# A tuned Fourier-mixing and gated-MLP kernel: one weight third loaded and folded inside stage 1, small pieces of work in other steps, the next batch's stage 2 earlier

## The chip, the cores and the metric

One core of a Trainium2 chip. The metric is the device time of one execution in microseconds (us). A profiled execution gives a trace of every engine; its time axis starts at the first instruction.

## The reference, cut to what matters

```python
# x: (8, 3008, 256); w_gate, w_val: (256, 1536); w_out: (1536, 256)
X = np.fft.fft(np.fft.fft(x, axis=1), axis=2).real.reshape(24064, 256)
out = (np.maximum(X @ w_gate, 0) * (X @ w_val)) @ w_out
```

## The kernel before

The sequence transform is done in two stages of matmuls (3008 = 94 x 32). The feature transform is folded into the weights: `wc` and `ws` are the cosine and sine transforms of W_gate and W_val, made on the chip in three thirds of 512 columns, four folds to each third (gate and value, cosine and sine). A fold is two small f32 matmuls into one PSUM buffer (PSUM is the memory that TensorE writes) and a cast of the result by ScalarE. In the start, the eight pieces of batch 0's stage 1 are done in groups, the lower half of the sequence first and the upper half when that part of x has come; the first evacuation of a piece copies its result out of PSUM. After the start, 288 steps run: 8 batches, 3 blocks, 12 slices of the hidden width. Each does the gate and value products (G and V in the traces), direct and mirrored; the output products follow 12 steps later. Steps 0 to 11 also do the remaining eight folds and the rest of batch 0's stage 2, in small pieces of matmul and copy: `upright` turns a block by a permutation (pst), `rotate` mends one column of it (psr), `stage2` makes a cosine or a sine half of a block's result (ps, copied to pq). The Nyquist row of each block is written to DRAM and read back, broadcast over 128 partitions (`nb`). The parts concerned:

```python
# start: x pieces of batch 0, then the first third of both weights (POOL's queue)
load_first(0, 8); ...; load_first(24, 8); ...; load_first(8, 4); load_first(20, 4)
...; load_first(12, 4); load_first(16, 4); ...
load_w(0, pl)
...
group((1, 2, 3), False); warm(9)      # lower half of stage 1; fillers: matmuls whose result nobody reads
...                                   # tables on ScalarE, copies of x on VectorE and ScalarE
group((1, 2, 3), True)                # upper half, then first_evac(1), (2), (3)
...
group((4, 5), False); warm(4); ...; group((4, 5), True)
...
group((6, 7, 0), False); first_evac(4, "act")
nc.sync.dma_start(out=seen[:], in_=t1t[0][0:1, 0, 8:10])   # waits for first_evac(4)
load_w(1, nc.sync); load_w(2, nc.sync)                     # second and third thirds
... pair_w(0, 0, dve)                 # sum and difference of the halves of W_gate's third
group((6, 7, 0), True)
...
fold_w(0, 0, 0, g_tile()); upright(0, 0, "act"); upright(0, 1, "dve"); fold_w(0, 0, 1, psw)
...                                   # rotation, two stage-2 halves, two more folds

def fold_w(n, i, cs, ps=None):
    ps = ps or spare("psw")           # spare: the two "o" buffers in turn
    ...                               # two f32 matmuls of 64 columns by 512
    nc.scalar.copy((wc, ws)[cs][i][:, sl_], ps[:])
    if cs and (n or i): scale_w(n, i, ps)     # VectorE reads the same buffer

# batch b+1: stage 1, shuffle through DRAM, rotation, stage 2, at these steps of batch b
sh, tr, t2 = (22, 28, (29, 30, 32, 34, 35, 37)) if b else (25, 30, (31, 32, 33, 34, 35, 37))
for i, k in enumerate(t2):
    at(t0 + k, stage2, b + 1, i // 2, i % 2, "act")   # cosine half, then sine half
```

## Time and profile before

| | before |
|---|---|
| time, median of 3 runs | 625.5 us (625.27 to 626.45) |
| span of the profiled run | 623.2 us |
| last stage-1 matmul of batch 0 starts | 15.10 us |
| first gate matmul starts | 21.18 us |
| first output matmul (step 12) starts | 50.36 us |
| from there to the end of the span | 572.8 us |

The last four rows cut the run into three stretches: start, steps 0 to 11, rest.

### The profile page before, as it was taken

To read this page: it belongs to the slowest core of one execution; us is meant where nothing else is said; L and a number is where in the kernel's file an instruction comes from. 1 tells how busy PE (TensorE), PEld (TensorE's weight loads), DVE (VectorE), ACT (ScalarE), POOL (GpSimd) and SP (SyncE) were. 2 spreads that over 40 slices of the span, in tenths; PEclk is the share of its full clock that TensorE was granted. 3 is DMA by queue.
4 is the path that set the end of the run, shared out by engine and by line. 5 is a ranking of instruction groups with operands and counts; after the bars stand their busy time and mean duration, and the time that the engine had idled before them with its cause. 6 is when DMAs were issued, how large, how long until landed. Compare 5 with 4: busy or idle time off the path is not lost.

```text
span 623.2 us, 11964 instructions
## 1 busy us (share of the span) xinstructions
PE 614.0 (99%) x4284; PEld 409.6 (66%) x4284; DVE 538.2 (86%) x654; ACT 444.6 (71%) x855; POOL 519.9 (83%) x447
## 2 busy tenths in 40 slices
PE   8999999999999999999999999999999999999996
PEld 5336666766666666666667666666666666666665
DVE  8677997899889898888988998898988889899991
ACT  8667777777777767767677767767677776766661
POOL 8987998998989898998989989898988865565665
PEclk9999999999999999999999999999999999999998
DMA  7885274525553183613825255531832134212114
GB/s 169 240 161 118 61 191 113 137 66 160 118 139 84 34 235 83 151 36 89 212 75 126 64 158 123 135 90 34 226 89 49 34 85 117 60 34 67 34 35 100
DMA packets 42038, 67.44 MB, mean 108 GB/s; under 512 B 5877, under 2 KB 31774, under 8 KB 39962
## 3 DMA queue, kind: packets, MB, share of 16 engines
q1 hardware_dynamic: 37162, 50.61, 32.3%
q0 software_dynamic: 4656, 15.88, 10.7%
q8 instruction: 33, 0.54, 0.4%
q14 instruction: 27, 0.22, 0.1%
q10 hardware_dynamic: 160, 0.20, 0.1%
HBM read 38.85 MB, written 30.17 MB: 111 GB/s over the span
## 4 chain that ended last, share of the span: by engine, by line
PE 96%; DVE 2%; ACT 1%; issue 0%; POOL 0%; POOLq 0%; DVEq 0%
PE po L683 40%; PE V L634 20%; PE G L619 10%; PE G L620 10%; PE G L626 10%; PE psw L333 2%; PE ps L162 2%; PE ps L271 2%; DVE h L647 0%; PE pst L240 0%; PE ps L216 0%; ACT t L230 0%; ACT back L197 0%; PE ps L166 0%; DVE wm L327 0%
## 5 line engine op out<-in xcount | busy, mean ns | idle before, releaser
L654 POOL TENSOR_TENSOR h<-gm,E 128x992 bf16<-128x992 f32 (+1 forms) x138 | 320.1, 2319 | 81.8 <-DVE E L661 50.4
L683 PE MATMUL po<-wo,h 128*128 128x256 bf16 (+2 forms) x2304 | 328.5, 272 | 0.0
L683 PEld LDWEIGHTS <-h 128*128 128x128 bf16 (+2 forms) x2304 | 231.4, 103 | 105.9
L628 ACT ACTIVATE gm<-G 128x496 f32<-128x496 f32 (+1 forms) x288 | 170.6, 592 | 94.6 <-PE G L626 87.8
L647 DVE TENSOR_TENSOR h<-gs,V 128x1024 bf16<-128x1024 f32 (+3 forms) x150 | 173.8, 1159 | 58.7 <-PE V L634 39.7
L641 DVE SCALAR_TENSOR_TENSOR E<-nb,af,V 128x496 f32<-128x496 bf16 (+1 forms) x276 | 190.2, 731 | 2.2 <-PE G L620 2.2
L621 ACT ACTIVATE gs<-G 128x497 f32<-128x497 f32 (+2 forms) x288 | 169.6, 589 | 24.7 <-PE G L620 24.7
L661 DVE SCALAR_TENSOR_TENSOR E<-E,V 128x992 f32<-128x992 f32 (+1 forms) x138 | 164.5, 1192 | 0.0
L619 PE MATMUL G<-pq,wc 128*128 128x497 bf16 (+2 forms) x288 | 107.9, 375 | 0.0
L620 PE MATMUL G<-pq,ws 128*128 128x497 bf16 (+2 forms) x288 | 107.9, 375 | 0.0
L626 PE MATMUL G<-pq,wm 128*128 128x496 bf16 (+1 forms) x288 | 107.9, 375 | 0.0
L634 PE MATMUL V<-pq,ws 128*128 128x497 bf16 (+2 forms) x288 | 85.4, 375 | 0.9 <-DVE E L641 0.9
L634 PE MATMUL V<-pq,wc 128*128 128x497 bf16 (+2 forms) x288 | 85.4, 375 | 0.0
L620 PEld LDWEIGHTS <-ws 128*128 128x128 bf16 x288 | 28.2, 98 | 32.7
L696 ACT COPY os<-po 128x512 f32<-128x512 f32 x63 | 37.0, 587 | 14.6 <-PE po L683 12.6
L634 PEld LDWEIGHTS <-wc 128*128 128x128 bf16 x288 | 28.2, 98 | 20.0 <-issue 1.6
L114 POOL TENSOR_TENSOR eo<-xla 94x256 bf16<-94x256 f32 x56 | 40.4, 733 | 0.7
L619 PEld LDWEIGHTS <-wc 128*128 128x128 bf16 x288 | 28.2, 98 | 18.1 <-DVE pq L278 0.8
L114 POOL TENSOR_TENSOR eo<-xlb 94x256 bf16<-94x256 f32 (+1 forms) x42 | 34.5, 822 | 0.9
L111 POOL TENSOR_TENSOR xla<-xla,xha 94x510 f32<-94x510 f32 x28 | 32.9, 1175 | 2.2
L177 ACT CAST t<-ps 96x512 bf16<-96x512 f32 x56 | 32.7, 584 | 2.4 <-PE ps L162 0.2
L626 PEld LDWEIGHTS <-wm 128*128 128x128 bf16 x288 | 28.1, 98 | 4.1 <-issue 1.6
(142 smaller groups left out, 370.8 us busy)
## 6 DMA issues: line engine op xcount, KB each, us to landing
out_dram<-os SPq DMA_DIRECT2D x124, 128.0 KB
Td<-t SPq DMA_DIRECT2D x7, 768.0 KB
t<-Td SPq DMA_DIRECT2D x7, 768.0 KB
out_dram<-os SPq DMA_DIRECT2D x82, 64.0 KB
xla<-in_x_dram SPq DMA_DIRECT2D x7, 720.0 KB
xlb<-in_x_dram SPq DMA_DIRECT2D x6, 640.0 KB
nb<-Nd SPq DMA_DIRECT2D x23, 128.0 KB
out_dram<-os SPq DMA_DIRECT2D x40, 48.0 KB
```

The source lines that it names most:

```text
L114: yield eng.tensor_tensor(e1[:, :, k:k + H], x1[:, :, 0:H], free(x1, D, [DX, n], [-1, H]), op=op)
L619: nc.tensor.matmul(G[:, ds], lhsT=wc[0][:, fs], rhs=pq[:, 0, ds], start=True, stop=False)
L620: nc.tensor.matmul(G[:, ds], lhsT=ws[0][:, fs], rhs=pq[:, 1, ds], start=False, stop=True)
L621: nc.scalar.activation(pair(t, "gs")[:, t % 2, ds], G[:, ds], ACTF.Relu)
L626: nc.tensor.matmul(G[:, cols], lhsT=wm[0][:, f * 128:(f + 1) * 128], rhs=pqt[b, blk][:, 1, cols], start=False, stop=True, skip_group_check ...
L628: nc.scalar.activation(pair(t, "gm")[:, t % 2, cols], G[:, cols], ACTF.Relu)
L634: nc.tensor.matmul(pair(t, "V")[:, t % 2, cs], lhsT=w[:, f * 128:(f + 1) * 128], rhs=pqt[b, blk][:, min(k, 1), cs], start=(k == 0), stop=( ...
L641: nc.vector.scalar_tensor_tensor(pair(t, "E")[:, t % 2, cols], nbt[b, blk][:, cols], af[:, f:f + 1], pair(t, "V")[:, t % 2, cols], op0=ALU ...
L647: nc.vector.tensor_tensor(pair(t, "h")[:, k, 0, 0:ds.stop - ds.start], pair(t, "gs")[:, k, ds], pair(t, "V")[:, k, ds], op=ALU.mult)
L654: eng.tensor_tensor(free(pair(t, "h")[:], 1024 * (t % 2) + 512 + w - 1, [1024, n], [-1, w]), pair(t, "gm")[:, k, cols], val[:, k, cols], o ...
L661: nc.vector.scalar_tensor_tensor(E[:, :, cols], E[:, :, cols], 2.0, V[:, :, cols], op0=ALU.mult, op1=ALU.subtract)
L683: nc.tensor.matmul(po[0:m, i, :], lhsT=pair(t - f + ff, "h")[:, ff % 2, sg, g * 128:g * 128 + m], rhs=wo[:, ff, :], start=(ff == 0), stop= ...
```

## The change

The intent: fold one quarter of the first weight third in a stretch where TensorE runs fillers anyway; arrange small pieces so that two folds do not wait for one buffer; and get the next batch's stage 2 ready sooner. Cut to its core:

```diff
         load_first(0, 8)
+        load_w(0, pl, (0,))
 ...
-        load_w(0, pl)
+        load_w(0, pl, (1,))
 ...
-        warm(9)
+        warm(11)
 ...
+        absolute(dq[:], da[:]); cosines(cd...); sines(cd...)   # moved up
         nc.scalar.copy(w1[:, 1:10, :], wn[:, 1, 1:10, :])
+        pair_w(0, 0, dve)
+        fold_w(0, 0, 0, g_tile())                              # both moved up
 ...
-    for n in (1, 2):
-        for k, t in enumerate(((0, 1, 2, 3), (4, 5, 6, 7))[n - 1]):
-            at(t, fold_w, n, k // 2, k % 2)
-    ... upright at 2, 4, 6, 8; rotate at 3, 7; stage2 at 5, 9, 10, 11
+    for n in (1, 2):   # folds at the same steps 0 to 7
+        ... upright at 1, 2, 4, 6; rotate at 2, 6 (ahead of the fold); stage2 at 3, 5, 7, 8
-    plan = {0: (12, 13, 14, 16, 19, 22, 23, 24), ...
+    plan = {0: (12, 13, 14, 15, 17, 20, 21, 22), ...
-        sh, tr, t2 = ... (25, 30, (31, 32, 33, 34, 35, 37))
+        sh, tr, t2 = ... (23, 29, (30, 31, 32, 34, 35, 37))
-            at(t0 + k, stage2, b + 1, i // 2, i % 2, "act")
+            at(t0 + k, stage2, b + 1, i // 2, 1 - i % 2, "act")
-            for half, k in enumerate((5, 24) if b else (14, 31)):
+            for half, k in enumerate((5, 24) if b else (14, 26)):
```

Further: 17 instead of 15 fold pieces of batch 1's x before the steps, a slower pace after, and POOL's second x load ahead of the first fold piece.

More of the change, by code (lines that the diff above doesn't have):

```diff
@@ L20 @@
 WARM = 12
-FIRST = 15
+FIRST = 17
 def view(ap, offset, dims):
@@ L409 @@
         pl.iota(pi[:], pattern=[[0, 1]], base=0, channel_multiplier=1)
+        iota(pl, mi[:], [[0, 1]], 0, 1)
+        iota(pl, free(dd[:], 0, [64, 2], [1, 64]), [[1, 2], [2, 64]], 0, 0)
         load_first(8, 4)
         load_first(20, 4)
-        iota(pl, mi[:], [[0, 1]], 0, 1)
-        iota(pl, free(dd[:], 0, [64, 2], [1, 64]), [[1, 2], [2, 64]], 0, 0)
         load_first(12, 4)
@@ L450, in group, with g_tile @@
                     first_products(c, upper, k)
+        def g_tile():
+            return psg.tile([128, 512], F32, tag="g", name="psw")
         angles(0, 9)
@@ L466 @@
         nc.scalar.mul(wn[:, 0, 9:16, :], wn[:, 1, 9:16, :], -1.0)
-        nc.scalar.copy(w1[:, 1:10, :], wn[:, 1, 1:10, :])
         back(0, 2, "dve")
@@ L470 @@
         residue(da[:], dq[:], D, dve)
-        jj, sl, up, odd = bits(0, 15), bits(4, 1), bits(5, 3), bits(0, 1)
+        absolute(dq[:], da[:])
+        cosines(cd[:, 0, 1:H], dq[:, 1:H], D)
+        sines(cd[:, 1, 1:H], da[:, 1:H], D, 1.0)
+        nc.scalar.copy(w1[:, 1:10, :], wn[:, 1, 1:10, :])
+        odd = bits(0, 1)
+        dve.tensor_copy(cd[:, 1, 0:1], odd[:])
+        dve.tensor_scalar(cd[:, 0, 0:1], odd[:], scalar1=-1.0, scalar2=1.0, op0=ALU.mult, op1=ALU.add)
+        pair_w(0, 0, dve)
+        fold_w(0, 0, 0, g_tile())
+        jj, sl, up = bits(0, 15), bits(4, 1), bits(5, 3)
         ends(24, 8)
@@ L496 @@
         dve.tensor_scalar(tabs["wzn"][:], wz[:, 0], scalar1=-1.0, scalar2=None, op0=ALU.mult)
-        dve.tensor_copy(cd[:, 1, 0:1], odd[:])
-        dve.tensor_scalar(cd[:, 0, 0:1], odd[:], scalar1=-1.0, scalar2=1.0, op0=ALU.mult, op1=ALU.add)
         dve.tensor_scalar(ui[:], ui[:], scalar1=up[:], scalar2=-1.0, op0=ALU.is_equal, op1=ALU.mult)
@@ L510 @@
         dve.tensor_scalar(tis[:], tis[:], scalar1=NB - 1, scalar2=None, op0=ALU.bitwise_and)
-        absolute(dq[:], da[:])
-        cosines(cd[:, 0, 1:H], dq[:, 1:H], D)
-        sines(cd[:, 1, 1:H], da[:, 1:H], D, 1.0)
         group((6, 7, 0), False)
@@ L520 @@
         first_evac(5, "act")
-        pair_w(0, 0, dve)
         for cs in range(2):
@@ L538 @@
         pl.tensor_scalar(ro[:, :, :, 0], di[:, :, :, 0], scalar1=0.0, scalar2=None, op0=ALU.is_equal)
-        def g_tile():
-            return psg.tile([128, 512], F32, tag="g", name="psw")
         pair_w(0, 1, pl)
@@ L545 @@
         pl.tensor_scalar(ix[:], ix[:], scalar1=0, scalar2=None, op0=ALU.max)
-        fold_w(0, 0, 0, g_tile())
+        psw = g_tile()
+        fold_w(0, 0, 1, psw)
         upright(0, 0, "act")
         upright(0, 1, "dve")
-        psw = g_tile()
-        fold_w(0, 0, 1, psw)
+        fold_w(0, 1, 0, g_tile())
         rotate(0, 0, 4, dve.tensor_copy)
@@ L553 @@
         stage2(0, 0, 0, "act")
-        fold_w(0, 1, 0, g_tile())
         stage2(0, 0, 1, "dve")
@@ L562 @@
             pair_w(2, i, pl)
+        load_x(1, 1, pl)
         first = fold(1, pl)
         next(first)
-        load_x(1, 1, pl)
         next(first)
@@ L745 @@
     for n in (1, 2):
-        for k, t in enumerate(((0, 1, 2, 3), (4, 5, 6, 7))[n - 1]):
-            at(t, fold_w, n, k // 2, k % 2)
-    for t, blk, cs, e in ((2, 1, 1, "dve"), (4, 1, 0, "dve"), (6, 2, 1, "dve"), (8, 2, 0, "dve")):
-        at(t, upright, blk, cs, e)
-    at(3, rotate, 0, 4, 8)
-    at(7, rotate, 0, 8, NKA)
-    for t, blk, cs, e in ((5, 1, 1, "act"), (9, 2, 1, "act"), (10, 1, 0, "dve"), (11, 2, 0, "act")):
-        at(t, stage2, 0, blk, cs, e)
+        t = 4 * n
+        at(t - 4, fold_w, n, 0, 0)
+        at(t - 3, fold_w, n, 0, 1)
+        at(t - 3 if n == 1 else t - 4, upright, n, 1, "act" if n == 1 else "dve")
+        at(t - 2, rotate, 0, 4 * n, 4 * n + 4)
+        at(t - 2, fold_w, n, 1, 0)
+        at(t - 2, upright, n, 0, "dve")
+        at(t - 1, fold_w, n, 1, 1)
+        at(t - 1, stage2, 0, n, 1, "act")
+        at(t + 1 if n == 1 else t, stage2, 0, n, 0, "act")
     at(8, nyquist)
-    plan = {0: (12, 13, 14, 16, 19, 22, 23, 24), 1: (4, 5, 7, 10, 14, 18, 20, 21)}
+    plan = {0: (12, 13, 14, 15, 17, 20, 21, 22), 1: (4, 5, 7, 10, 14, 18, 20, 21)}
     for b in range(B - 1):
@@ L761 @@
             at(t0 + k, stage1, b + 1, c, "act")
-        sh, tr, t2 = (22, 28, (29, 30, 32, 34, 35, 37)) if b else (25, 30, (31, 32, 33, 34, 35, 37))
+        sh, tr, t2 = (22, 28, (29, 30, 32, 34, 35, 37)) if b else (23, 29, (30, 31, 32, 34, 35, 37))
         at(t0 + sh, shuffle, b + 1)
@@ L774, in pace @@
     def pace(t):
-        paced["due"] += 0 if t < 12 else 0.8 if t < 23 else 0.75 if t < 54 else 23 / 36
+        paced["due"] += 0 if t < 12 else 0.75 if t < 22 else 0.68 if t < 54 else 23 / 36
         while paced["due"] >= 1:
```

## The prediction

> **What bounds the kernel now.** I read the page's busy lines first, then busy time by stretches, then the chain that ended last in its first 22 us, then the timeline of each engine up to 110 us, then the waits after 50 us. The stretches (busy us, in brackets instructions, of PE, PEld, DVE, ACT, POOL; then granted clock, DMA share, GB/s):
>
> ```profile
> 12.00:15.20 3.20, 3.10 (x38) 2.80 (x35) 2.09 (x8) 2.44 (x9) 2.82 (x7) 1.00 0.81 280
> 15.20:21.20 6.00, 6.00 (x37) 2.15 (x35) 4.64 (x9) 4.00 (x8) 4.92 (x6) 1.00 0.80 253
> 21.20:42.60 21.40, 21.15 (x104) 7.01 (x103) 15.04 (x25) 14.08 (x29) 18.84 (x22) 1.00 0.76 183
> 42.60:50.00 7.40, 6.63 (x53) 3.54 (x53) 6.31 (x12) 4.93 (x10) 7.01 (x12) 1.00 0.84 134
> 100.00:105.00 5.00, 4.14 (x32) 2.76 (x30) 3.35 (x4) 2.87 (x6) 2.86 (x4) 1.00 0.49 147
> 105.00:600.00 495.00, 495.00 (x3475) 337.51 (x3474) 443.57 (x494) 361.78 (x692) 415.51 (x322) 1.00 0.40 100
> ```
>
> From 105 to 600 us TensorE has work in every microsecond. Nothing in the diff removes a matmul there, so only three places can move the end: the start (to 21.2 us, where the first gate matmul begins), the first twelve steps (to about 50 us), and one hole near 102 us. The last 23 us (17.54 busy) are untouched. Who owns the hole, from the waits after 50 us (who waited for whom: us, times, longest):
>
> ```profile
> PE V L634 <- DVE E L641: 0.9, 1, 0.9
> DVE E L641 <- PE G L620: 2.2, 3, 1.8
> ```
>
> The DVE instruction E reads nb, the Nyquist row of the next batch broadcast by DMA. The queue of SyncE shows the row's write issued at 92.76 us and the broadcast at 98.68; E starts at 101.65. So the name "G" in the second line is the wrong releaser: those matmuls were long done, the DMA was last. Of the early part, the chain (start, length, what):
>
> ```profile
> 5.42 0.53 ACT tq L365
> ...
> 8.29 0.80 ACT w L467
> 9.09 1.12 ACT back L197 x3
> 10.22 1.27 ACT t L230 x3
> 11.49 0.56 ACT back L197
> 12.05 0.22 ACT dq L365
> 12.27 0.02 issue
> 12.29 0.40 ACT cd L362
> 12.69 0.20 ACT cd L358
> 12.89 0.43 ACT t L230
> 13.32 0.04 issue
> 13.36 0.24 PE ps L216
> ```
>
> ScalarE, without a pause from 5.42 to 13.32 us, sets when TensorE gets the last stage-1 group; TensorE meanwhile runs filler matmuls. VectorE is nearly as full (3.75 of 5 us between 10 and 15), and the DMA engines are 0.8 to 1.0 busy: three resources are close to binding.
>
> **What the Trainium skill says.** (1) "DMA: Bandwidth & Descriptors", section on queues, rings and completion order: each DMA engine consumes descriptors in ring order. The trace agrees as far as it goes: x pieces and weights land in the order of issue (x at 5.9 us and 12.5 us, then W_gate's third just before 14.2, W_val's just before 16.0). A load put between pieces of x therefore pushes the later pieces back. (2) "FP8 and Floating Point Precision", TensorE Precision Notes: true FP32 takes 4 passes. A fold (two 64-column f32 products of 512) occupies 1.01 us in the trace, against 0.21 us for a bf16 matmul of 496. (3) "TensorE: Matmul & The Clock Gate", part 1: an idle TensorE is throttled. The clock is 1.00 in each stretch above, so fillers hold it, and two more of them in a wait cost nothing. (4) "Perfetto Trace Analysis", Identifying the Most-Contended Engine: matmul busy time is no measure of headroom. I therefore compared starts of successive matmuls with their usual spacing: between 105 and 600 us less than 0.2 us is lost in each 10 us, so that stretch has no hidden holes either.
>
> **The change part by part.**
>
> A. Load and early fold. Two 256 KB loads go in behind the first x piece. Between 11.5 and 15.5 us the 1 MB of weight thirds flowed in 3.9 us, so half of it takes about 1.9 us: later x pieces land 1.7 to 1.9 us later (the last at 14.3, not 12.5). Issue on POOL (0.6 us each) shifts by 1.2, which hides under that. VectorE gets the pair sums (2 x 0.69, about 1.4 us) and the two cd columns (0.14) ahead of the second x piece, whose work began at 8.69; with three of four bit extractions behind them that work begins near 10.4, 1.7 later. ScalarE gets Abs, cosine, sine before the w copy (0.84, later removed: neutral), and the cast of the fold (0.5). That cast needs the fold: VectorE finishes da at 7.7, the columns at 8.2, the differences at 9.6; from operand to cast took 1.17 us (15.63 to 16.80), so the cast starts at 10.8 while ScalarE is free at 9.9. Its x copies start at 11.3 instead of 9.0. By the first-evacuation of group 4 (12.89 before) the 0.84 has come back, but TensorE's own order, pieces 4 and 5, then four fillers (0.86), then the upper half, makes it 14.5. The last stage-1 group then ends near 16.9 instead of 15.2: +1.7. So all three resources ask for the same delay.
>
> Back: the first fold is gone from the place after stage 1. It held TensorE from 15.27 to 16.69, 1.42 us with its wait for the pair differences. From 15.27 to the first gate at 21.18 there were 5.91 us; without that fold 4.5. VectorE's queue there (evacuation, m2 twice at 0.63, upright at 0.68, rotation) now lags the shorter TensorE work: upright ready near 19.85, rotation 0.3 late, its copy another 0.2, which gives back about 0.5. Sum of A: 1.7 - 1.42 + 0.3 = +0.6 us at the first gate.
>
> B. Steps 0 to 11. A step with a fold is bound by TensorE: folds start at 22.25, 24.62, 26.99 (2.37 apart). Adding an upright or a stage-2 half adds 0.22 (29.58 - 26.99 = 2.59). A step without a fold takes 1.78 (44.57, 46.35, 48.13) whatever small piece is in it, since it goes round V, mirror product on DVE, direct product on DVE, V; TensorE waits 0.27 in it. Before, steps 0 to 7 hold three uprights and one stage-2 half; after, four uprights and three halves: 3 x 0.22 = +0.66, moved out of steps 8 to 11 where they were free. Steps 9 to 11 do not get shorter by it. In return the turns of the two o buffers change. Before, the fold waited for the scaled copy at 32.23 (0.24), at 37.46 (0.05), and the upright at 42.61 (0.15): 0.44. A buffer comes free about 1.56 us after its fold; with a half or upright in between (0.23 + 1.25 + 0.09 = 1.57) two of these waits vanish, one of about 0.2 stays (step 6, where only the rotation separates). -0.25. Step 8 loses 0.08 of DVE work. Sum of B: +0.3 us.
>
> C. Batch change. Sine halves of stage 2 first, and at step 30 instead of 32: the row goes out two steps (4.3 us) earlier, and the x load that sat in the queue before it (89.30, which explains the 5.6 us wait for the row's write) is five steps earlier. The hole of 0.85 us should go: -0.85. Later batches had no wait there: 0.
>
> D. Fold pieces: POOL waited 1.48 us for x at 32.36 and then issued the b-half load for 2.6 us; exchanging them fills the wait, so 17 pieces should be done near 51.6, where 15 ended at 51.1. The lower pace then emits about one piece less by step 54; stage 1 still finds its pieces two steps ahead. No TensorE time: 0.
>
> E. Fillers 9 to 11: 0.43 us inside the wait for the fold: 0.
>
> Sum: +0.6 + 0.3 - 0.85 = +0.05 us, or 625.5. The diff bears marks of tuning (the exact filler count, the reordered turns), which speaks for something gained that I cannot derive; I put the middle half a microsecond lower, at 625.0.
>
> **Rivals.** R1: stage 1 is not delayed by 1.7 but by 0.5 or less, because ScalarE and VectorE had slack that the trace's chain hides; then A is -0.6 and the time 624.2. For it: x pieces 2 to 4 may have landed before they were used. Against: ScalarE has no gap from 5.42 to 13.32. R2: W_gate lands late (after 8.2 us), the pair sums and the cast stall VectorE and ScalarE at once, and everything behind them slips: each microsecond of lateness is one at the end; 626.5. Against: it is second in the ring, and the first piece was in at 5.9. R3: the new wait moves: the hole at 102 us shrinks only partly because the row still waits in the SyncE queue behind output stores; 625.9 instead. For it: stores stand ahead of it in the new order. R4: slower fold pieces leave stage 1 of each later batch waiting for POOL (0.89 busy): 6 batches by 0.5 us would be +3. Against: no TensorE wait for POOL shows anywhere after 50 us.
>
> **Range and chances.** A is uncertain by 1 us either way, B by 0.4, C by 0.2, with R4 as a small tail: 623.3 to 626.7. Two per cent is 12.5 us, more than all early waits together; faster 1%, same 98%, slower 1%.
>
> **What would show it.** A: last stage-1 matmul near 16.9 us, first gate near 21.7; the first fold at 9.4 to 10.5. B: fold starts in steps 3 to 7 about 2.6 apart, the step-8 piece near 20.8 us after the fold of step 0 (20.4 before), steps 9 to 11 still 1.78. C: no TensorE wait near 102 us. D: no TensorE wait on POOL. The prediction is wrong if the first gate starts before 21 us or after 22.7, if steps 9 to 11 are shorter than 1.7, or if a wait shows in later batches.

## The result, and the profile after

Ratios here and below are the mean time of one kernel's fast runs over that of the kernel before in the same rounds, so not quite the ratio of the medians. The changed kernel took 626.42 us (625.72 to 627.25, 4 runs) against 625.49; ratio 1.0012, interval 0.9995 to 1.003. Again it gave 1.0011 (0.9997 to 1.0024). It is the same by the 2% measure; the medians say 0.9 and 0.25 us slower (625.78 against 625.53 the second time). That it is slower by about 0.7 us rests on the two traces, which agree, and not on the intervals.

| | before | after | after, again |
|---|---|---|---|
| last stage-1 matmul | 15.10 | 17.50 | 17.55 |
| first gate | 21.18 | 22.12 | 22.17 |
| first gate to first output | 29.18 | 29.96 | 29.83 |
| first output to end of span | 572.8 | 571.8 | 571.8 |
| span | 623.2 | 623.9 | 623.8 |

So 0.94 us was lost in the start and 0.78 in the steps, and 1.0 won at the batch change. The chain that ended last, of the changed kernel (start, length, what), shows how stage 1 got longer:

```profile
9.74 1.24 PE psw L333 x4
10.98 0.02 issue
11.00 0.59 ACT wc L336
11.59 1.12 ACT back L197 x3
12.71 0.41 ACT t L230
13.12 0.04 issue
13.16 0.66 PE ps L216 x6
13.81 0.06 issue
13.87 0.81 PE psk L398 x3
14.68 0.51 PE ps L216 x6
```

Where the chain before was ScalarE alone, it now goes from the early fold (psw) to its cast (wc), to ScalarE's x copies (back) that stand behind the cast, to the first evacuation (t), which frees the buffer that piece 5 needs, to the four fillers (psk; this trace holds three of them, that of the second run all four), and only then to the upper half of pieces 4 and 5. ScalarE's own timeline of the changed kernel gives the size of the wait (in brackets: idle before, and what ended it):

```profile
8.90 0.90 ACT L477 COPY w<-wn 94x864 bf16<-94x864 bf16 x1
11.00 0.59 ACT L336 CAST wc<-psw 128x512 bf16<-128x512 f32 x1 [1.21 <-PE psw L333]
```

The stretches that the prediction opened with, in the changed kernel (same columns):

```profile
12.00:15.20 3.20, 2.57 (x23) 2.01 (x25) 1.99 (x12) 2.39 (x6) 2.99 (x7) 1.00 0.76 205
15.20:21.20 6.00, 5.88 (x57) 3.53 (x56) 2.77 (x7) 4.66 (x11) 4.30 (x7) 1.00 0.50 161
100.00:105.00 5.00, 5.00 (x39) 3.40 (x38) 4.08 (x5) 3.73 (x7) 4.08 (x4) 1.00 0.40 108
105.00:600.00 495.00, 493.58 (x3449) 337.48 (x3474) 443.25 (x493) 361.76 (x692) 415.02 (x322) 1.00 0.39 100
```

Between 12 and 15.2 us TensorE is now idle for 0.6 us, where it was idle for 0.1; the hole in 100 to 105 is filled. The 1.4 us missing in the long stretch are no wait: weight loads are as many as before (3474), matmul records 26 fewer, so some records are missing from this trace.

In the steps, TensorE's timeline, first before, then after, shows the mirrored value products of steps without a fold:

```profile
45.73 0.37 PE L634 MATMUL V<-pq,wm 128*128 128x496 bf16 x1
47.51 0.37 PE L634 MATMUL V<-pq,wm 128*128 128x496 bf16 x1
```

```profile
47.45 0.37 PE L636 MATMUL V<-pq,wm 128*128 128x496 bf16 x1 [0.24 <-DVE h L649]
49.23 0.37 PE L636 MATMUL V<-pq,wm 128*128 128x496 bf16 x1 [0.37 <-DVE h L649]
```

1.78 us apart in both. Before, each of these steps also held a stage-2 half; after, none does, and the freed time shows as a wait for VectorE.

### The profile page after: what moved, and what is told of

The parts are those of the page before. It is cut to its first block, busy times and chain, and to the rows that moved or that the text cites. A ratio compares the mean times of both kernels' runs of the same rounds, so it can differ in the third digit from the quotient of the medians.

```text
span 623.9 us, 11933 instructions
## 1 busy us (share of the span) xinstructions
PE 612.6 (98%) x4254; PEld 409.7 (66%) x4286; DVE 535.7 (86%) x652; ACT 445.5 (71%) x857; POOL 521.2 (84%) x447
## 3 DMA queue, kind: packets, MB, share of 16 engines
HBM read 38.85 MB, written 30.17 MB: 111 GB/s over the span
## 4 chain that ended last, share of the span: by engine, by line
PE 96%; DMA 1%; issue 1%; DVE 1%; ACT 1%; POOL 0%; POOLq 0%; DVEq 0%
PE po L685 40%; PE V L636 19%; PE G L621 10%; PE G L628 10%; PE G L622 10%; PE psw L333 2%; PE ps L162 2%; PE ps L271 2%; DMA lo<-in_x_dram 1%; PE ps L216 1%; PE psk L398 1%; DVE h L649 0%; PE pst L240 0%; PE ps L166 0%; ACT back L197 0%
## 5 line engine op out<-in xcount | busy, mean ns | idle before, releaser
L621 PE MATMUL G<-pq,wc 128*128 128x496 bf16 (+2 forms) x287 | 107.6, 375 | 1.2
L636 PE MATMUL V<-pq,ws 128*128 128x496 bf16 (+2 forms) x280 | 83.7, 374 | 0.0
L636 PE MATMUL V<-pq,wc 128*128 128x496 bf16 (+2 forms) x266 | 80.7, 374 | 0.0
L698 ACT COPY os<-po 128x512 f32<-128x512 f32 x63 | 37.0, 587 | 14.3 <-PE po L685 12.5
```

What stands on the lines that cost most here:

```text
L621: nc.tensor.matmul(G[:, ds], lhsT=wc[0][:, fs], rhs=pq[:, 0, ds], start=True, stop=False)
L636: nc.tensor.matmul(pair(t, "V")[:, t % 2, cs], lhsT=w[:, f * 128:(f + 1) * 128], rhs=pqt[b, blk][:, min(k, 1), cs], start=(k == 0), stop=( ...
```

## The experiments

Eleven runs were made beyond the first two; one is the changed kernel again, the other ten stand in the table. It gives the times from TensorE's timeline, then the ratio to the kernel before and the median. "Rest" is from the first output matmul to the end of the span. The kernels before ran at medians of 625.55, 625.3 and 625.53 us in the three calls.

| kernel | last stage 1 | first gate | steps | rest | median | ratio (95%) |
|---|---|---|---|---|---|---|
| a_start | 17.82 | 22.44 | 30.17 | 573.1 | 626.33 | 1.0006 (0.9992 to 1.002) |
| b_steps | 15.91 | 21.46 | 29.83 | 572.9 | 626.0 | 1.0009 (0.9995 to 1.0023) |
| c_batch | 15.58 | 21.22 | 29.18 | 572.0 | 624.22 | 0.998 (0.9967 to 0.9994) |
| c_order | 15.75 | 21.29 | 29.18 | 572.4 | 625.1 | 0.9993 (0.9979 to 1.0007) |
| after_nofill | 16.64 | 21.35 | 29.84 | 571.8 | 625.05 | 0.9997 (0.9984 to 1.0011) |
| after_latecast | 16.78 | 21.41 | 29.83 | 572.0 | 625.04 | 1.0002 (0.9988 to 1.0016) |
| c_turns | 15.93 | 21.47 | 28.75 | 571.9 | 623.85 | 0.9979 (0.9965 to 0.9992) |
| best_mix | 16.33 | 21.29 | 29.50 | 571.9 | 624.45 | 0.9981 (0.9967 to 0.9995) |
| load_only | 16.15 | 21.68 | 29.18 | 572.6 | 625.99 | 1.0009 (0.9995 to 1.0022) |
| mix_seen | 16.08 | 21.80 | 28.75 | 572.0 | 623.95 | 0.9975 (0.9961 to 0.9988) |

One thing to learn from the first column: five profiles have the same start (before, b_steps, c_batch, c_order, c_turns), as far as the program goes, and their last stage-1 matmul starts between 15.10 and 15.93 us, mean 15.65; their first gate between 21.18 and 21.47, mean 21.32. The profile that the prediction was read from is the earliest of the five. The new start (after twice, a_start) has means 17.62 and 22.24. Against these means the start loses 0.92 us. A single profile can therefore be off by some tenths at the first gate, and by more before it.

### The three parts, each alone

a_start is the kernel before with the new start only; b_steps with the new steps 0 to 11 only; c_batch with the new plan for batch 1 and the earlier fold pieces only. Each takes the change's own lines for its part and none for the others.

> Part A alone on the kernel before (early load of W_gate's first third, its cosine fold inside stage 1, 11 fillers; the rest as before). Theory (parts add): the last stage-1 matmul ends 2.4 us later than before and 1.5 us come back, so the first gate starts at 22.1 us as in the changed kernel (before 21.2) and the time is 0.9 us above before, with the hole near 102 us still there (0.85). Rival (part A gains and the loss lies in the steps or at the batch change): first gate at 21.2 or earlier, time equal to before or below.

> Part B alone (uprights, rotations, stage-2 halves of batch 0 in other steps). Theory: three more small pieces in steps that TensorE fills, none gained in steps 9 to 11: from first gate to gate of step 12 29.5 us instead of 28.75, time +0.6 to +0.8 us. Rival (the new turns remove the waits for buffers and pay for it): 28.75 or less, time equal or below.

> Parts C and D alone (stage 1, shuffle, rotation and stage 2 of batch 1 earlier, sine halves first, 17 fold pieces, slower pace). Theory: the hole near 102 us (0.85 us) goes and nothing else moves: time 0.85 us below before, no TensorE wait after 50 us. Rival (earlier work only moves the wait, or fold pieces come late): time equal to before, a TensorE wait elsewhere after 50 us.

The parts do add as the theory said in each stretch: first gate 22.44 with the new start alone, steps 29.83 with the new steps alone, rest 572.0 with the new batch plan alone. a_start brought something unexpected: its steps took 30.17, not 29.18. The fold of step 0 took 2.07 us instead of 1.08, since POOL's pair sums of the second weight third stood 2.14 us waiting for its load (POOL's timeline of a_start):

```profile
21.83 1.27 POOL L321 TENSOR_TENSOR wst<-wst 128x512 f32<-128x512 f32 x1 [2.14 <-DMA wst<-in_moe_w_gate_dram]
```

That load is released by the evacuation of piece 4, so a later stage 1 also delays the weights. In the changed kernel the same wait of POOL is 1.27 us and costs TensorE 0.12 (a fold of 1.20 us); in its second run it is 1.15 us and the fold takes 1.08. The times of a_start and b_steps alone are within noise of the kernel before (intervals include 1); their traces are the evidence. c_batch is faster by time too: its interval ends at 0.9994. Its median is 1.3 us below the kernel before, of which its trace shows 0.8.

A second surprise: in a_start and b_steps TensorE does not wait at 102 us, though their batch plan is the old one. Their waits, one line each of the waits of a_start and of b_steps (who for whom: us in total, times, longest):

```profile
PE psr L259 <- DMA t<-Td: 0.9, 1, 0.9
```

```profile
PE psr L259 <- DMA t<-Td: 0.8, 1, 0.8
```

The rotation of batch 1 waits at 90 us for the shuffle through DRAM. load_only (below), whose batch plan is the old one too, waits there for 0.18 us and not at 102. In b_steps and load_only VectorE still waits for the broadcast row (0.63 and 0.85 us), but TensorE is not stopped by it. The rest takes 572.6 to 573.1, as in the kernel before. We read this as one shortage that shows up at either of two places, which no run tests by itself; what stands firm is the sum: the four profiles with the old batch plan have a rest of 572.85 on average, the eight with the whole new one 571.8 to 572.0.

### Only the order of the halves

```diff
-            at(t0 + k, stage2, b + 1, i // 2, i % 2, "act")
+            at(t0 + k, stage2, b + 1, i // 2, 1 - i % 2, "act")
```

> Only the order of the two stage-2 halves exchanged (sine half first), all steps as before. Theory (the row of batch 1 comes too late because its half is second): the row goes out one step (2.1 us) earlier, the hole of 0.85 us is gone: time 0.85 below before. Rival (the row's write sits behind the x load and the stores in the queue, whenever it is issued): hole keeps half or more of its 0.85 us.

Half of each: the row goes out 2 us earlier (90.78 us), VectorE reads it at 100.37 without a wait, where it waited 0.6 to 1.8 us in three of the four profiles with the old order (before 1.77, load_only 0.85, b_steps 0.63), and TensorE's wait at 102 us is gone. But the rotation waits 0.3 us for the shuffle, and the rest takes 572.4, midway between 572.8 and 572.0. That 0.3 is not the exchange's doing, which acts only from step 31 on: the rotation is in step 30, and with the old plan the same wait is 0 to 0.9 us. SyncE's queue tells why the full plan does better; first before, then c_batch (start, time in the queue, what is sent):

```profile
75.14 2.61 SPq L734 DMA_DIRECT2D out_dram<-os  x6
77.84 0.86 SPq L252 DMA_DIRECT2D Td<-t  x1
92.76 0.24 SPq L282 DMA_DIRECT2D Nd<-pq  x1
98.68 0.35 SPq L283 DMA_DIRECT2D nb<-Nd  x1
```

```profile
73.06 0.31 SPq L252 DMA_DIRECT2D Td<-t  x1
77.83 4.13 SPq L734 DMA_DIRECT2D out_dram<-os  x6
89.43 0.23 SPq L282 DMA_DIRECT2D Nd<-pq  x1
91.78 0.34 SPq L283 DMA_DIRECT2D nb<-Nd  x1
```

Before, the shuffle's write (Td) stands behind six output stores; with the new plan it leaves ahead of them, 4.8 us earlier. The row (Nd to nb) goes out 3.3 us earlier and its broadcast 6.9 us earlier: it follows the row's write after 2.4 us instead of 5.9. The x load, just ahead of the row before (89.30), now goes at 82.08. How much of this the x load alone makes is not separated: in c_order it goes behind the row, and the broadcast still follows after 3.9 us.

### What lengthens stage 1

Two edits of the changed kernel. after_nofill:

```diff
         group((4, 5), False)
-        warm(4)
```

> The changed kernel without the four filler matmuls between the lower and the upper half of pieces 4 and 5. Theory (with the early fold TensorE reaches these fillers after the data is ready, so they lie on the path): the upper half of pieces 4 and 5 starts 0.65 to 0.85 us earlier (13.9 us instead of 14.5), the first gate at 21.4 instead of 22.1, time 0.7 us below the changed kernel (625.7). Rival (the late x pieces set the end of stage 1): first gate at 22.1, time unchanged.

after_latecast, with the fold's matmuls left where they are:

```diff
-        fold_w(0, 0, 0, g_tile())
+        (the two matmuls only, into ps0)
 ...
         for c in (1, 2, 3):
             first_evac(c, "act")
+        nc.scalar.copy(wc[0][:, 0:512], ps0[:])
```

> The changed kernel with ScalarE's cast of the early fold moved behind the three first evacuations, matmuls unmoved. Theory (ScalarE stood 1.2 us waiting for that fold, in order, and all its later copies with it): its x copies start near 10.5 us instead of 11.5, the first evacuation at 11.9 instead of 12.6, first gate 0.7 us earlier (21.4), time 0.7 us below the changed kernel. Rival (VectorE's pair sums in front of the x work set it): x copies earlier, but first gate unchanged at 22.1.

Both came out as the theory said: first gate 21.35 and 21.41 instead of 22.12. ScalarE's timeline of after_latecast shows the copies ahead of the cast:

```profile
9.74 0.71 ACT L197 COPY back<-hi 94x381 bf16<-94x381 bf16 x2
11.88 1.30 ACT L230 CAST t<-ps 128x384 bf16<-128x384 f32 x3 [0.73 <-PE ps L216]
```

The copies start 1.7 us earlier than in the changed kernel, the first evacuation 0.7 earlier; the difference is now a wait for TensorE. So the cast and the fillers are two links of one chain, and taking out either gives 0.7 us. The two gains do not add: with both out (best_mix, below) the last stage-1 matmul is at 16.33 and the first gate at 21.29. Both rivals fall, that late x and that VectorE's pair sums set the end of stage 1. But x is close behind: in after_nofill VectorE waits 0.65 us for the last x piece, which it takes at 14.01. Without the four fillers the granted clock stayed at 1.00 in every stretch of the start.

load_only leaves the fold and everything else in the old place and moves only the load:

```diff
         load_first(0, 8)
+        load_w(0, pl, (0,))
 ...                          # two iotas of POOL moved ahead of load_first(8, 4), as in the change
-        load_w(0, pl)
+        load_w(0, pl, (1,))
```

> Only the place of the load: W_gate's first third asked for behind the first x piece, the fold and everything else where the kernel before has it. Theory (the load itself costs little, the placing of the work on ScalarE and VectorE cost 1.6 of the 2.4 us): the last x piece is used near 13.5 to 14.0 us instead of 12.5, last stage-1 matmul 0.5 to 0.9 us later than before (15.6 to 16.0), the wait of the first fold (0.36) goes, first gate 0.2 to 0.5 us later, time +0.2 to +0.5. Rival (the load pushes the x pieces and that is what costs): last stage-1 matmul at 17 us or later, first gate +1 us or more.

The last stage-1 matmul is at 16.15, 0.5 us after the mean of the old starts and a little beyond what was expected; the first gate at 21.68 is 0.36 above their mean of 21.32. So of the 0.92 us of the start, some 0.36 is the load and 0.56 is where the work was put; with one profile of load_only against five that spread over 0.29 us, this is an estimate. ScalarE now really waits for x (its timeline of load_only):

```profile
9.45 0.71 ACT L197 COPY back<-hi 94x381 bf16<-94x381 bf16 x2 [0.56 <-DMA hi<-in_x_dram,ixf]
10.55 0.61 ACT L197 COPY back<-lo 94x508 bf16<-94x508 bf16 x1 [0.39 <-DMA lo<-in_x_dram]
```

### The changed kernel again

> The changed kernel once more, for its ratio on the chip of the runs beside it. Theory: parts add, 1.0 at the first gate, 0.7 in the steps, -0.85 at the batch change, so 0.1 to 0.2% above the kernel before (626.2), first gate near 22.2 us. Rival: its higher times so far are noise, ratio 1.000.

As told above: ratio 1.0011, first gate 22.17. Its interval just includes 1, so by time alone the rival is not excluded.

### Versions built from the theory

c_turns is c_batch with the old steps, but in steps 3, 5 and 7 the order turned:

```diff
+    at(3, rotate, 0, 4, 8)             # registered, and so run, ahead of the folds
+    at(5, stage2, 0, 1, 1, "act")
+    at(7, rotate, 0, 8, NKA)
     for n in (1, 2):
         for k, t in enumerate(...): at(t, fold_w, n, k // 2, k % 2)
```

> Parts C and D on the kernel before, with the small pieces left in their old steps, but in steps 3, 5 and 7 the rotation or stage-2 half ahead of the fold, so that two folds never follow each other in one buffer. Theory: the waits for the scaled copy at the folds of steps 4 and 6 and at the upright of step 8 (0.24, 0.05, 0.15) go without any piece being moved: first gate to step 12 28.3 us instead of 28.75, time 0.4 us below parts C and D alone (624.2), so 623.8. Rival (these waits are not the buffers'): 28.75, 624.2.

The steps took 28.75 instead of 29.18 us: 0.43 less, with no piece moved to another step. (The expectation's 28.3 and 28.75 count to the gate of step 12, the table to the first output matmul.) The fold of step 4, before and in c_turns, on TensorE's timeline:

```profile
29.58 1.08 PE L333 MATMUL psw<-wst,cd 128*64 128x512 f32 x4
32.23 1.08 PE L333 MATMUL psw<-wst,cd 128*64 128x512 f32 x4 [0.17 <-DVE wm L327]
```

```profile
29.88 1.08 PE L333 MATMUL psw<-wst,cd 128*64 128x512 f32 x4
32.25 1.08 PE L333 MATMUL psw<-wst,cd 128*64 128x512 f32 x4
```

2.65 us apart before, 2.37 after; 0.04 of this is the rotation, which c_turns has ahead of the first of the two. By time, c_turns is ahead of c_batch by 0.4 us of medians; the trace decides, not the intervals.

best_mix adds to this the early load and fold with the late cast and without the four fillers.

> The version that the theory would build: early load and early fold with the late cast and without the four fillers, old steps with the turns of the run before, parts C and D. Theory: first gate 1.4 us before the changed kernel's (20.7, and 0.6 before the kernel before's), 28.3 us to step 12, no hole: 623.2 us or less, below both kernels by over 2 us. Rival (the early fold costs as much as it saves however it is placed): first gate at 21.2 or later, time 623.8 or more.

It beats both kernels by about 1 us, but not c_turns. The theory failed and the rival's numbers came out: first gate at 21.2 or later, 623.8 us or more. The first gate came at 21.29, no better than the mean of the old starts, and the fold of step 0 took 1.83 us, because POOL waited 1.54 us for the second weight third. mix_seen lets that load go earlier:

```diff
-        nc.sync.dma_start(out=seen[:], in_=t1t[0][0:1, 0, 8:10])
+        nc.sync.dma_start(out=seen[:], in_=t1t[0][0:1, 0, 6:8])
```

> The mixed version with the loads of the second and third weight thirds let go by the evacuation of group 3 instead of group 4. Theory (in the mixed version the fold of step 0 took 1.83 us because its pair sums on POOL waited 1.54 us for the second third, and these loads start late): POOL's pair sums start 1 us earlier (19.5 instead of 20.45), the fold of step 0 takes 1.1 us, first gate to step 12 28.75 us instead of 29.5, time 0.7 us lower than the mixed version (623.7). Rival (the transfers are limited by bandwidth, an earlier start only slows x): last x piece later than 14.0, first gate later by about what step 0 wins, time unchanged at 624.4.

Neither theory holds whole. POOL's sums start at 19.37 and the steps take 28.75, as expected; x is not later (13.64 against 14.01). But the first gate moved from 21.29 to 21.80. The fold of W_val's third, on TensorE's timeline of best_mix and of mix_seen:

```profile
18.16 1.41 PE L333 MATMUL psw<-wst,cd 128*64 128x512 f32 x4
```

```profile
17.90 2.18 PE L333 MATMUL psw<-wst,cd 128*64 128x512 f32 x4
```

The wait went to an earlier fold, whose differences POOL finished at 18.96 instead of 18.44. This is not a later load: POOL's timelines, best_mix and mix_seen, show its work on that third begin at nearly the same time and the difference take longer; why, no run shows.

```profile
15.81 1.28 POOL L321 TENSOR_TENSOR wst<-wst 128x512 f32<-128x512 f32 x1 [0.39 <-DMA wst<-in_moe_w_val_dram]
17.17 1.27 POOL L323 TENSOR_TENSOR wst<-wst 128x512 f32<-128x512 f32 x1
```

```profile
15.88 1.28 POOL L321 TENSOR_TENSOR wst<-wst 128x512 f32<-128x512 f32 x1 [0.59 <-DMA wst<-in_moe_w_val_dram]
17.24 1.72 POOL L323 TENSOR_TENSOR wst<-wst 128x512 f32<-128x512 f32 x1
```

In both versions, then, folds from 18 us on wait for POOL's sums, in one for the load of the second third, in the other for POOL itself. The medians (624.45, 623.95) and spans (622.7, 622.5) differ by little.

## Why the prediction was right or wrong, point by point

The time (625.0, range 623.3 to 626.7, "same") held: the measured 626.42 lies in the range, 1.4 above the point. The sum of the parts, +0.05, gave 625.5; the half microsecond taken off for marks of tuning was wrong and had nothing measured behind it. The class was safe whatever the parts did: 2% is 12.5 us. The parts sum to +0.7 in the traces, and A and B were both too small; that the time still lay near the point is partly luck.

- **A, the start: right in sign, too small.** Predicted +0.6, measured +0.94 against the same profile and +0.92 against the means. The mis-sized term is the delay of stage 1: +1.7 predicted, +2.4 measured against that profile, 2.0 against the mean of five. The ScalarE part was close: copies at 11.3 predicted, 11.48 measured. What was missed is TensorE's wait for the buffer of piece 5 (0.53 us until 13.16), which puts the lower half of 4 and 5 and the four fillers after the first evacuation: the evacuation of piece 4 came at 15.21, not at 14.5. The statement that "all three resources ask for the same delay" failed: with the new start VectorE took the last x piece at 13.46 without a wait (in after_nofill at 14.01 after one), not at 14.3. The page quoted under (1) says ring order of the queues of SyncE and ScalarE; x and these weights went by POOL's queue, and load_only is what shows that the load pushes x there. The sum of A has a slip: the text works out about 0.5 given back by VectorE's lag and adds 0.3; with 0.5 A would have been +0.8. The return after stage 1 was 1.46 us against that profile, more than the 1.1 predicted (1.42 less 0.3); against the mean of old starts it is 1.05 (5.67 before, 4.62 after), since in the other four profiles the first fold hardly waits.
- **B, the steps: right mechanism, too small.** Predicted +0.3; measured +0.65 (b_steps, and the changed kernel's second run) to +0.78 (its first, with 0.12 of the late fold of step 0). The three moved pieces (0.66) were right, and steps without a fold stayed at 1.78. From fold to fold, the changed kernel against the one before, step 1 takes 2.67 instead of 2.37 us, step 4 2.82 instead of 2.59, and step 7, to its first value product, 1.90 instead of 1.67; the other steps from 2 to 6 are the same within 0.01. The order costs nothing: TensorE's timeline of the changed kernel has 0.52 us from a value product to the fold with a stage-2 half between, 0.30 without, so the half adds 0.22 ahead of a fold as behind it.

```profile
30.64 0.37 PE L636 MATMUL V<-pq,ws 128*128 128x496 bf16 x1
30.94 1.08 PE L333 MATMUL psw<-wst,cd 128*64 128x512 f32 x4
35.88 0.37 PE L636 MATMUL V<-pq,ws 128*128 128x496 bf16 x1
36.09 0.39 PE L271 MATMUL ps<-m,t 128*128 128x128 bf16 x4
36.40 1.08 PE L333 MATMUL psw<-wst,cd 128*64 128x512 f32 x4
```

  The mis-sized term is what would come back: 0.33 was predicted (0.25 from the buffers, 0.08 in step 8), under 0.1 came. The wait at the fold of step 4 shrank from 0.24 to some 0.05, and the one wait predicted to stay did so, 0.2 us at the fold of step 6. But step 8, from the first value product of step 7 to its own, took 2.12 instead of 2.21 us: only 0.09, where 0.15 of a wait and 0.08 of work should have gone. There the value product now follows the gate product after 0.35 us instead of 0.21.
- **C, the batch change: right.** -0.85 predicted; -0.8 (c_batch) and -1.0 (the changed kernel) measured against the one profile before, -0.95 between the means of four and eight profiles. That the row was late for the order of its halves is shown by c_order, where VectorE no longer waits for it. That the shuffle was as short of time was not seen; the change's earlier shuffle covers it, and a_start and b_steps show its wait under the old plan.
- **D, E: right.** No TensorE wait on POOL after 50 us in any run with the new pace. The two added fillers lie in the wait for the fold, whose second product began when the differences were done (9.84).
- **Rivals.** R1 (a small delay of stage 1) fell. R2 (late W_gate) fell: VectorE took it at 8.43 without a wait. R3 and R4 did not occur.

So the expected gain of the early fold went three ways: to the load that pushes x (some 0.36), to work put in front of x in the queues of ScalarE and VectorE and to fillers that then lay on the path (some 0.56 more than came back), and, once these were mended, to later folds that wait for POOL's sums. What remains open is how much of the 0.36 is bandwidth and how much POOL's later issue (its last x load went out at 8.51 in load_only, 7.39 before), and why POOL's difference took longer in mix_seen.

## What to carry to other kernels

Work moved into a wait of one engine must also fit the queues of the others, which here ran in the order of the program: here the fold filled TensorE's wait, but its cast stopped ScalarE for 1.21 us ahead of copies that everything needed. Before moving a piece, ask whether its old place cost anything: pieces in steps bound by another loop (1.78 us) were free, and the same pieces in steps bound by TensorE cost 0.22 each. Where two users of a pair of buffers alternate, swapping the order inside a step (0.43 us) can do what moving work to other steps did not.

## What the Trainium skill lacked or had wrong

- "DMA: Bandwidth & Descriptors", latency: it gives a floor for tiny transfers. On a queue shared with loads and stores the 1 KB row took 5.6 us from issue to the broadcast behind it; in c_order, with no x load ahead but stores, 3.9 (90.78 to 94.66, start to start); in c_batch the next rows took 1.1 us (93.02 to 94.15, and 98.83 to 99.92). A transfer of one size took from 1.1 to 5.6 us here, which the floor alone does not foretell.
- "TensorE: Matmul & The Clock Gate", back-to-back issue gap: it gives no time for f32 operands. A fold of two 64-column f32 products of 512 held TensorE 1.01 us, and a matmul ahead of a fold kept it 0.30 us instead of 0.21.
- "Perfetto Trace Analysis", identifying the most-contended engine: apart from the clock's warm-up, no page says how much one profile can differ from another of the same instructions. Five profiles of one start placed its last stage-1 matmul between 15.10 and 15.93 us and the first gate between 21.18 and 21.47. Against the one profile the delay of stage 1 and the return after it are both 0.4 us larger than against the mean; in A they cancel (0.94, 0.92).
